# A table of 1237 numbers takes over the order in which a fused attention and MLP-mixer kernel emits its operations

## The chip, the cores and the metric

The kernel runs on one core of a Trainium2 chip. The metric is the device time of one execution in microseconds (us). A core has TensorE (PE in the profile, its weight loads PEld), VectorE (DVE), ScalarE (ACT), GpSimd (POOL) and SyncE (SP), which here issues every DMA. Each engine works through its own instructions in the order in which the program lists them and waits on semaphores for the others.

A difference of about 0.2% (0.8 us) is what a measurement of this kernel can tell from no change.

## The reference

```python
x  = A_x                                   # 1 x 2048 x 512
xn = layernorm(x)
s  = A_ref(xn, A_wqkv, A_wo)               # sliding local attention, 32 heads of 16, 8 keys at distance 2
g  = silu(B_ref(xn, B_w1, B_b1, B_w2, B_b2))   # layernorm, 512 -> 1376, gelu, -> 512
return x + s * g
```

In `A_ref` each position s looks at keys and values s, s-2, ..., s-14; scores are scaled by 1/4, masked where the index is negative, and softmaxed over the eight. `B_ref` layer-normalises its input a second time.

## The kernel before

The 2048 positions are split into even and odd ones (`DIL = 2`, index `c`), each half into `NI = 8` tiles of 128 rows, and the 32 heads into `NHB = 4` groups of 8 (index `hb`). All matmuls are fp16 pairs: a number is a high and a low half, a product is three matmuls (high by high, low by high, high by low), so each operand is first scaled by a power of two, rounded (`hi`) and its remainder computed (`lo`).

- **Start.** `load` issues the DMAs of x, the qkv weights and w1. Row statistics of each x tile are taken on DVE (`ln0`, L576, L577, L631); POOL raises them to the power -1/2 (L635); `y0` applies them (L661 on ACT, L665 on POOL, L668 on DVE), transposes the tile on PE (L683) and writes its halves to `yT` (L687, L689, L690), or sends it through a DMA transpose (L675). For tiles 6 and 7 `direct` multiplies centred x by unrounded weights in fp32 (L617). `scale_q` takes sums of squares of a weight group on ACT (L514), PE adds them over the partitions (L430), DVE makes the scale (L441 to L459); `prep_q` writes the weight halves (L536 on ACT, L543 on DVE, L470 and L471 on POOL). While PE has nothing to do, 24 matmuls on a constant run (`WAKE`, L1169).
- **Eight units** (`c`, `hb`). `qkv` fills U[u % 2] with 8 tiles of 12 matmuls of 384 columns (L746), each scaled out of PSUM by ACT (L763) or DVE (L759), then DMAs on SP build the halo of the neighbouring rows (L771). `attention` runs almost wholly on DVE in instructions of 2048 elements a partition (L805, L808, L863, L858), with its softmax exp on ACT and parts of its sums on POOL (L873, L883).
- **MLP** of four chunks of 512 rows, 11 slices f each, poured between the units: `mlp1` (12 matmuls, L1016), gelu and high half on ACT (L1033, L1036), low half on DVE (L1038), `mlp2` (12 matmuls into the four banks z0 to z3, L1052), silu on ACT (L1063, L1068), and for three chunks a store to scratch (`gd`). The weights w2 get their scale from sums of squares on ACT (L421, L1232) which PE adds over the partitions (L435).
- **End.** `wo_first` multiplies the even half by `wo` (L929). `wo_last` does the odd half (L961) in nine parts, seven tiles and the last one in two halves: nine matmuls of the first three head groups, then three of the last; DVE multiplies by the gate (L993), DVE or POOL adds x (L1000, L997), SP stores the tile (L1002). The x tiles of this stage are loaded by L983 into the seven-buffer ring `R_f`.

What sets the order: every step is handed to a planner (`Plan.add`) with an engine, an assumed duration, its reads and writes and a priority. `Plan.issue` then simulates the engines: each time it takes the operation that can start first by the assumed durations, priority breaking near ties, gives it buffers of its rings, and notes it. At the end the operations are emitted in that order; a ring buffer goes to the operation that comes first in this order.

Of the kernel before, what the change touches and what calls it, by code (L numbers as in the profile page):

```python
# [66 lines left out]
W2LATE = 6  # L67

BEFORE_W1 = (0, 1, 4, 5)

class Buf:

# [24 lines left out]
class Plan:  # L97
# [9 lines left out]
    def add(self, eng, dur, fn, reads=(), writes=(), prio=None, table=None, nbytes=0,  # L107
# [14 lines left out]
        o.n = len(self.ops)  # L122
        o.eng, o.dur, o.fn, o.table, o.nbytes = eng, dur, fn, table, nbytes
        o.port, o.rate, o.issue, o.tail = port, rate, issue, tail
        o.prio = self.prio if prio is None else prio
        o.preds, o.succs, o.bufs = set(), [], []
# [95 lines left out]
    def issue(self):  # L222
        self.start()
        engs = {o.eng: [] for o in self.ops}
        for o in self.ops:
            if not o.npred:
                engs[o.eng].append(o)
        order = []
        while len(order) < len(self.ops):
            best = None  # L230
            for e, cand in engs.items():
                lst = []
                for o in cand:
                    t = self.earliest(o)
                    ok = True
                    for b in o.bufs:
                        if b.slot is None:
                            f = min(b.ring.free)
                            if f == float("inf"):
                                ok = False  # L240
                                break
                            t = max(t, f)
                    if ok:
                        lst.append((t, o))
                if lst:
                    t0 = min(x[0] for x in lst)
                    t, o = min((x for x in lst if x[0] <= t0 + (WINDOW if x[1].prio > PURG else WURG)),
                               key=lambda x: (x[1].prio, x[1].n))
                    if best is None or (t, o.prio) < (best[0], best[1].prio):
                        best = (t, o)  # L250
            if best is None:
                raise RuntimeError("no operation can be placed")
            t, o = best
            engs[o.eng].remove(o)
            for b in o.bufs:
                if b.slot is None:
                    r = b.ring.free
                    b.slot = r.index(min(r))
                    r[b.slot] = float("inf")
            end = self.place(o, t)  # L260
            for b in o.bufs:
                b.left -= 1
                b.end = max(b.end, end)
                if not b.left:
                    b.ring.free[b.slot] = b.end
            for x in self.done(o, end, MARGIN):
                engs[x.eng].append(x)
            order.append((t, o))
        self.end = max(self.free.values())
        for t, o in order:  # L270
            o.fn()
# [1095 lines left out]
```

## Time and profile before

| | |
|---|---|
| median of 3 runs | 414.9 us (414.75 to 414.92) |
| time of the profiled execution | 415.18 us |
| its span, first to last instruction | 413.4 us |
| mean granted TensorE clock | 0.999 |
| busy PE / DVE / ACT / POOL | 405.9 / 379.5 / 222.1 / 120.3 us |
| DMA moved | 46.41 MB |

The span is 1.8 us under the profiled execution's time. A busy time counts a stretch once even where instructions overlap. In a list of waits each row gives the waiting engine and line, what released it, and the total, count and longest of the waits. In a timeline, a row starts with start and duration in us, merges equal neighbours (x4), and puts the idle time before it and its releaser in brackets.

### The profile page before, as it was taken

How to read it: one execution, taken by the hardware profiler on the slowest of the kernel's cores; microseconds unless marked ns; L12 is line 12 of the kernel's file. 1: busy time of each engine (PE TensorE's matmuls, PEld its weight loads, DVE VectorE, ACT ScalarE, POOL GpSimd, SP SyncE). 2: the span in 40 equal slices, each digit the busy share in tenths (PEclk: the TensorE clock that was granted, in tenths of full speed). 3: DMA queues.
4: the chain of work that ended last, by engine and by line, in shares of the span. 5: the costliest groups of instructions: out<-in, count | busy, mean ns of one | idle time of the engine just before them, and what ended most of it. 6: DMA issues, size and time to landing. Idle time of an engine off the chain costs nothing.

```text
span 413.4 us, 5554 instructions
## 1 busy us (share of the span) xinstructions
PE 405.9 (98%) x2083; PEld 206.6 (50%) x2083; DVE 379.5 (92%) x379; ACT 222.1 (54%) x353; POOL 120.3 (29%) x131
## 2 busy tenths in 40 slices
PE   8799999999999999999999999999999999999996
PEld 5555544445654455445544554455455544444443
DVE  4996989998999999989998999999999998999954
ACT  4699899994549655843384252225212393263500
POOL 3834002004380425042504330434033404520021
PEclk9999999999999999999999999999999999999999
DMA  8958717030045137720172034223604244007133
GB/s 281 397 112 258 235 61 230 0 128 1 1 142 152 28 93 183 149 46 2 48 221 75 0 102 116 68 86 88 205 7 122 88 111 145 0 18 238 23 102 131
DMA packets 47211, 46.41 MB, mean 112 GB/s; under 512 B 31785, under 2 KB 32225, under 8 KB 46673
## 3 DMA queue, kind: packets, MB, share of 16 engines
q1 hardware_dynamic: 47184, 46.06, 37.6%
q8 instruction: 16, 0.26, 0.3%
q14 instruction: 11, 0.08, 0.1%
HBM read 24.06 MB, written 7.34 MB: 76 GB/s over the span
## 4 chain that ended last, share of the span: by engine, by line
PE 92%; ACT 3%; issue 1%; DVE 1%; POOL 1%; ACTq 0%
PE z L1052 28%; PE ps L1016 28%; PE ps L746 25%; PE ps L929 5%; PE ps L961 2%; PE z L961 2%; PE pl L746 1%; ACT w L421 1%; PE pl L961 1%; ACT f L673 1%; ACT yT L687 0%; ACT wq L536 0%; POOL wq L471 0%; POOL rb L635 0%; ACT prod L661 0%
## 5 line engine op out<-in xcount | busy, mean ns | idle before, releaser
L1016 PE MATMUL ps<-yT,w 128*128 128x512 f16 (+1 forms) x528 | 120.4, 379 | 0.0
L746 PE MATMUL ps<-wq,yT 128*128 128x384 f16 x708 | 117.0, 326 | 0.2 <-DVE U L759 0.2
L1052 PE MATMUL z<-w,h 128*128 128x512 f16 x480 | 110.4, 379 | 0.0
L746 PEld LDWEIGHTS <-yT 128*128 128x128 f16 x744 | 72.5, 98 | 49.2 <-issue 1.0
L1016 PEld LDWEIGHTS <-w 128*128 128x128 f16 (+1 forms) x528 | 52.8, 100 | 61.0
L805 DVE TENSOR_TENSOR prod<-U 128x2048 f32<-128x2048 f32 x32 | 73.2, 2286 | 2.2 <-POOL prod L883 0.7
L1052 PEld LDWEIGHTS <-h 128*128 128x128 f16 x480 | 46.6, 98 | 55.5 <-issue 0.3
L808 DVE TENSOR_REDUCE L<-prod 128x128 f32<-128x2048 f32 x32 | 73.0, 2281 | 0.4
L1033 ACT ACTIVATE ps<-ps,b1T,hsc 128x512 f32<-128x512 f32 (+1 forms) x44 | 32.9, 748 | 73.4 <-PE ps L1016 72.2
L863 DVE TENSOR_TENSOR prod<-pl,U 128x2048 f32<-128x2048 f32 x28 | 63.2, 2283 | 4.2 <-POOL prod L873 4.1
L763 ACT ACTIVATE U<-ps,cs 128x384 f32<-128x384 f32 x54 | 31.2, 580 | 65.2 <-PE ps L746 65.2
L873 POOL TENSOR_TENSOR prod<-prod,prod 128x2048 f32<-128x2048 f32 x7 | 31.7, 4531 | 113.8 <-DVE prod L863 99.6
L883 POOL TENSOR_TENSOR prod<-prod 128x1024 f32<-128x1024 f32 x14 | 32.9, 2349 | 0.0
L882 POOL COPY gate<-prod 1x1 f32<-1x1 f32 x21 | 5.5, 264 | 91.0 <-DVE prod L805 82.2
L1038 DVE SCALAR_TENSOR_TENSOR h<-ps,hsc,h 128x512 f16<-128x512 f32 x40 | 29.6, 741 | 1.7 <-ACT h L1036 1.4
L1036 ACT ACTIVATE h<-ps,hsc 128x512 f16<-128x512 f32 x40 | 27.3, 684 | 1.3 <-PE z L1052 0.4
L929 PE MATMUL ps<-wo,oT 128*128 128x512 f16 x96 | 21.7, 379 | 0.0
L858 DVE TENSOR_TENSOR prod<-prod,prod 128x2048 f32<-128x2048 f32 x9 | 20.5, 2282 | 0.0
L1033 ACT ACT_TABLE_LOAD x10 | 12.8, 1283 | 8.6 <-PE ps L1016 8.5
L883 POOL TENSOR_TENSOR prod<-prod,prod 128x1024 f32<-128x1024 f32 x7 | 16.4, 2347 | 0.0
L961 PEld LDWEIGHTS <-oT 128*128 128x128 f16 x108 | 10.6, 98 | 10.4
L929 PEld LDWEIGHTS <-oT 128*128 128x128 f16 x96 | 9.4, 98 | 11.2
(179 smaller groups left out, 377.8 us busy)
## 6 DMA issues: line engine op xcount, KB each, us to landing
f<-in_A_x_dram SPq DMA_DIRECT2D x31, 256.0 KB, 3.5
U<-U SPq DMA_DIRECT2D x16, 392.0 KB, 4.0
gd<-f SPq DMA_DIRECT2D x12, 256.0 KB, 3.4
prod<-in_A_x_dram SPq DMA_DIRECT2D x8, 256.0 KB, 6.9
oT<-in_B_w_dram SPq DMA_DIRECT2D x2, 1024.0 KB
yT<-in_B_w_dram SPq DMA_DIRECT2D x2, 1024.0 KB, 7.9
f<-gd SPq DMA_DIRECT2D x8, 256.0 KB, 2.7
out_dram<-f SPq DMA_DIRECT2D x8, 256.0 KB, 2.8
```

The costliest lines, as they stand in the source:

```text
L746: nc.tensor.matmul(b.t[:, 0:384], y[:, s, k, o:o + P], wq[:, hb, t, k], start=(n == 0), stop=(n == 11))
L763: act(384, lambda i=i, b=b: nc.scalar.activation(U3[:, i:i + 31:15, :], b.t[:, 0:384].rearrange("p (t e) -> p t e", t=3), AF.Identity, sca ...
L805: dve(2048, lambda p2=p2, g=g: nc.vector.tensor_tensor(p2(), q, slots(Ut, KH, 2 * g), op=ALU.mult), qk + [("kh", ub, 0), ("kh", ub, 1), (" ...
L808: dve(2048, lambda pr=pr, g=g: nc.vector.tensor_reduce(L3()[:, 2 * g:2 * g + 2], pr.t.rearrange("p (r f d) -> p r f d", r=2, d=DH), AX.X, ...
L863: dve(2048, lambda: nc.vector.tensor_tensor(pr.t.rearrange("p (r f d) -> p r f d", r=2, d=DH), A3()[:, 2 * g:2 * g + 2].rearrange("p r (f ...
L873: pool(4.75, lambda: nc.gpsimd.tensor_tensor(acc.t, acc.t, p1.t, op=ALU.add), [acc, p1], [acc])
L883: nc.gpsimd.tensor_tensor(x.t[:, 0:1024], x.t[:, 0:1024], y(), op=ALU.add)
L929: nc.tensor.matmul(b.t, oT[:, hb, i // 4, s, i % 4], wo[:, t, hb], start=(hb == 0 and n == 0), stop=(hb == last and n == 2))
L961: nc.tensor.matmul(b.t[:, cols], oT[:, hb, i // 4, s, i % 4], wo[:, t, hb, cols], start=(start and hb == 0 and n == 0), stop=(stop and hb ...
L1016: nc.tensor.matmul(b.t[0:M], w1[:, s, f * 512 + k * M:f * 512 + (k + 1) * M], yT[ch][:, t, k], start=(n == 0), stop=(n == 11))
L1033: act(512, lambda: nc.scalar.activation(b.t[0:M], b.t[0:M], AF.Gelu_apprx_tanh, bias=b1T[0:M, f:f + 1], scale=hsc[0:M, 1:2]), [b, ("b1T",) ...
L1052: nc.tensor.matmul(z.t, hl[s][0:K, t * P:(t + 1) * P], w2[0:K, w, f], start=(f == 0 and n == 0), stop=(f == NF - 1 and n == 2))
```

## The change

`ORDER` lists all 1237 operations of the planner by number. `Plan.issue` takes them one after the other from this table in place of choosing; the choosing loop is then never entered. Operations, their durations for the planner, shapes, engines and data are the same. What differs is the order on each engine's queue, and which buffer of a ring an operation gets.

```diff
+ORDER = (
+    0, 1, 19, 2, 3, 4, 5, 6, 7, 8, 9, 10, 33, 32, 108, 116, 115, 130, 111, 124, 110, 114, 129, 112, 127, 20,
...
+    1197, 893, 1216, 1202, 1232, 1207, 1222, 1212, 1227, 1236, 1217,
+)
...
-        order = []
+        order, fixed = [], [self.ops[n] for n in reversed(ORDER)]
         while len(order) < len(self.ops):
             best = None
-            for e, cand in engs.items():
+            if fixed:
+                o = fixed.pop()
+                t = max([self.earliest(o)] + [min(b.ring.free) for b in o.bufs if b.slot is None])
+                assert not o.npred and t < float("inf")
+                best = (t, o)
+            for e, cand in engs.items() if best is None else ():
```

The line numbers of the changed kernel are 64 higher than before up to `Plan.issue` and 69 higher behind it (L514 is L583, L993 is L1062). Three places follow.

ACT at the start. `prod_93` holds the weights of the first head group, `U_87` those of the second, `wq` the fp16 weights; `z_146` is the PSUM bank with the transposes of x tile 0, and `yT_82` receives it. Before:

```order
L514 ACT_TABLE_LOAD
L514 ACTIVATE wq,s_122<-prod_93 128x768 x2
L536 ACTIVATE wq<-prod_93,qsc 128x384 x4
L514 ACTIVATE wq,s_124<-U_87 128x768
L687 CAST yT_82<-z_146 128x4x128
L514 ACTIVATE wq,s_124<-U_87 128x768
L659 ACTIVATE rb_151<-pb_150,rb_151 128x1
```

The same queue now:

```order
L583 ACT_TABLE_LOAD
L583 ACTIVATE wq,s_121<-prod_93 128x768 x2
L605 ACTIVATE wq<-prod_93,qsc 128x384 x2
L583 ACTIVATE wq,s_123<-U_87 128x768
L605 ACTIVATE wq<-prod_93,qsc 128x384
L583 ACTIVATE wq,s_123<-U_87 128x768
L605 ACTIVATE wq<-prod_93,qsc 128x384
L756 CAST yT_82<-z_146 128x4x128
```

Both sums of squares of the second head group now stand ahead of the fourth weight chunk of the first group and of the first cast of x.

DVE at the end. `ps`, `z` are PSUM banks, `U_86` holds gate, product and result of the odd half, `f` the x tiles; rows of 128x256 are the halves of the last tile. Before:

```order
L993 SCALAR_TENSOR_TENSOR U_86<-z_144,osc,U_86 128x512
L1000 TENSOR_TENSOR U_86<-U_86,f_101 128x512
L993 SCALAR_TENSOR_TENSOR U_86<-z_145,osc,U_86 128x512
L1000 TENSOR_TENSOR U_86<-U_86,f_102 128x512
L993 SCALAR_TENSOR_TENSOR U_86<-z_146,osc,U_86 128x256
L1000 TENSOR_TENSOR U_86<-U_86 128x256
L993 SCALAR_TENSOR_TENSOR U_86<-ps_139,osc,U_86 128x256
L1000 TENSOR_TENSOR U_86<-U_86 128x256
```

Now:

```order
L1062 SCALAR_TENSOR_TENSOR U_86<-ps_139,osc,U_86 128x256
L1069 TENSOR_TENSOR U_86<-U_86 128x256
L1069 TENSOR_TENSOR U_86<-U_86,f_96 128x512
L1069 TENSOR_TENSOR U_86<-U_86 128x256
L1062 SCALAR_TENSOR_TENSOR U_86<-z_145,osc,U_86 128x512
L1069 TENSOR_TENSOR U_86<-U_86,f_100 128x512
```

The last part is now a whole tile (bank z20, tile 6) and no longer half a tile; PE's last twelve matmuls are likewise those of bank z20, with 512 columns, and no longer those of bank ps0, with 256.

SP at the end. `o160` goes through a DMA transpose into `oT` for the last head group; rows of `out_0_dram` are the stores. Before:

```order
L983 DMA f5_101<-in_A_x_dram 128x512
L983 DMA f6_102<-in_A_x_dram 128x512
L983 DMA U0_86<-in_A_x_dram 128x512
L851 DMA_TRANSPOSE oT_88<-o160_105 128x8x128 x2
L1002 DMA out_0_dram<-U0_86 128x512 x7
L1002 DMA out_0_dram<-U0_86 128x256 x2
```

Now:

```order
L920 DMA_TRANSPOSE oT_88<-o160_105 128x8x128 x2
L1052 DMA f3_99<-in_A_x_dram 128x512
L1071 DMA out_0_dram<-U0_86 128x512
L992 DMA out_0_dram<-f1_97 128x512
L1071 DMA out_0_dram<-U0_86 128x512
L1071 DMA out_0_dram<-U0_86 128x256
L1071 DMA out_0_dram<-U0_86 128x512 x4
L1071 DMA out_0_dram<-U0_86 128x256
L1071 DMA out_0_dram<-U0_86 128x512
```

A store of the even half (L992, from buffer f1) has moved to the end, so one buffer of the ring is missing and the load of an x tile into f3 (tile 4) has moved behind the transposes, where it must wait for the add that reads the x tile now in f3. The last three stores are those of tile 6, of the second half of tile 7, and of tile 4; by the table they stand in this order, so the store of the part that is computed last is no longer the last of the queue: two more stand behind it.

58 rows, old and new, of the table ORDER are left out of this document.

## The prediction

> **What bounds the kernel now.** I read the page's engine shares first, then PE's waits, then the busy times by stretches.
>
> ```profile
> PE 405.9 (98%) x2083; PEld 206.6 (50%) x2083; DVE 379.5 (92%) x379; ACT 222.1 (54%) x353; POOL 120.3 (29%) x131
> ...
> PE z L683 <- POOL prod L665: 1.6, 1, 1.6
> PE z L683 <- DVE prod L668: 0.4, 1, 0.4
> PE ps L746 <- DVE U L759: 0.2, 1, 0.2
> ...
> L1169 PE MATMUL z<-fours 128*128 128x256 bf16 x24 | 5.3, 389 | 1.2 <-DVE fours L365 1.2
> ...
> 0.00:10.00 10.00, 8.61 (x35) 5.20 (x36) 4.43 (x15) 4.23 (x8) 3.39 (x12) 1.00 0.80 277
> 10.00:20.00 10.00, 7.87 (x47) 5.19 (x48) 9.57 (x29) 6.42 (x14) 8.16 (x9) 1.00 1.04 411
> 20.00:30.00 10.00, 9.81 (x61) 5.73 (x59) 9.72 (x25) 9.97 (x17) 4.73 (x4) 1.00 0.48 105
> 30.00:120.00 90.00, 89.92 (x474) 45.77 (x472) 82.64 (x103) 70.30 (x133) 22.05 (x24) 1.00 0.37 116
> 120.00:160.00 40.00, 39.96 (x210) 20.35 (x208) 38.84 (x29) 26.82 (x43) 13.11 (x14) 1.00 0.40 103
> 160.00:240.00 80.00, 80.00 (x416) 40.76 (x414) 75.67 (x55) 42.51 (x61) 24.84 (x26) 1.00 0.34 86
> 240.00:360.00 120.00, 120.00 (x610) 59.78 (x609) 116.70 (x88) 45.41 (x60) 36.19 (x33) 1.00 0.33 98
> 360.00:400.00 40.00, 40.00 (x187) 18.45 (x186) 34.59 (x31) 16.45 (x21) 5.70 (x11) 1.00 0.29 80
> 400.00:414.00 14.00, 9.76 (x58) 5.39 (x55) 7.36 (x12) 0.00 (x0) 2.16 (x2) 0.95 0.41 150
> ```
>
> PE is the bound. In the windows the first number is the length and the next PE's busy time: from 30 to 400 us it is busy 369.88 of 370 us, although DVE is close behind it (348.4 us of the same 370). PE's waits are the three rows of 1.6, 0.4 and 0.2 us and the 1.2 us before the first constant matmul, 3.4 us in all. The 24 constant matmuls (5.3 us) fill holes of the start. An order can't shorten the matmuls; so from 30 to 400 us a new order can only lose, and what can be won is at the start (those waits, and holes that the constant matmuls cover) and behind the last matmul.
>
> **The start.** Two chains must meet before PE's stream of L746 can run: x tile 0 (statistics, POOL, transposes, cast) and the four high chunks of the first weight group.
>
> ```profile
> 8.32 0.13 DVE L441 TENSOR_SCALAR ssq<-z 128x1 f32<-128x1 f32 x1
> ...
> 8.80 0.68 DVE L576 BATCH_NORM_STATS2 bn<-prod 128x6 f32<-128x512 f32 x1
> 9.52 0.18 DVE L577 BATCH_NORM_AGGREGATE mv<-bn 128x2 f32<-128x6 f32 x1
> ...
> 8.92 2.13 ACT L536 ACTIVATE wq<-prod,qsc 128x384 f16<-128x384 f32 x4 [1.15 <-DVE qsc L459]
> 10.96 0.83 ACT L514 ACTIVATE wq<-U 128x768 bf16<-128x768 f32 x1
> ...
> 13.55 0.59 ACT L687 CAST yT<-z 128x512 f16<-128x512 f32 x1 [1.67 <-PE z L683]
> 14.03 0.85 ACT L514 ACTIVATE wq<-U 128x768 bf16<-128x768 f32 x1
> ...
> 17.25 0.54 DVE L668 TENSOR_SCALAR prod<-prod,mv,rb 128x512 f32<-128x512 f32 x1
> ...
> 10.73 2.08 POOL L665 TENSOR_SCALAR prod<-prod,mv,rb 128x512 f32<-128x512 f32 x1
> ...
> 12.86 0.66 PE L683 MATMUL z<-ident,prod 128*128 128x128 f32 x4 [1.65 <-POOL prod L665]
> 13.35 2.75 PE L617 MATMUL z<-prod,U 128*128 128x384 f32 x8
> ...
> 15.96 0.81 PE L746 MATMUL ps<-wq,yT 128*128 128x384 f16 x4
> ...
> 17.84 1.85 PE L683 MATMUL z<-ident,prod 128*128 128x128 f32 x12 [0.40 <-DVE prod L668]
> ...
> f<-in_A_x_dram SPq DMA_DIRECT2D x31, 256.0 KB, 3.5
> U<-in_A_wqkv_dram SPq DMA_DIRECT2D x2, 384.0 KB
> ```
>
> Now tile 0's statistics come ahead of the weight scale on DVE: they start at 8.32 in place of 8.80, so POOL's L665 ends at about 12.81 - 0.45 = 12.4 and the transposes are 0.45 us early. The scale pays: its first instruction (L441) starts 0.9 us of statistics and 0.1 us behind 8.32, at 9.3, and so the first L536 at 8.92 + 1.0 = 9.9. From there ACT's new order runs two L536 (2 x 0.53), L514 (0.9 with its read-out), the third L536: 12.4. Then stands the second L514, which needs the last load of the second weight group. That load is the twelfth: eight tiles of x of 256 KB and four pieces of weights of 384 KB are 3.67 MB, of which 2.77 MB move in the first 10 us at 277 GB/s and the rest at 411 GB/s, an estimate of 12.2 us. The trace shows it present at 14.03. I take the middle, 13.1. So L514 runs 13.1 to 14.05, the fourth L536 to 14.6, the cast to 15.2, where before it ended at 14.14.
>
> PE's first L746 needs that cast: 15.2 against 15.96 before. But PE has by then done only four of the eight instructions of L617 on bank z; the other four (1.3 us) follow, so it stands at 15.2 + 1.3 = 16.5 where before it stood at 15.96: 0.55 us behind. Two constant matmuls that now stand in the full stream add 0.2 us each. Against this the waits of 0.40 and 0.2 us and the 0.1 us that the windows lack from 30 us on go: tile 2's normalisation (L668) no longer stands behind four others on DVE, nor its POOL step behind the weight remainder, and is done at about 15 in place of 17.79. Sum 0.55 + 0.4 - 0.7 = **+0.3** with rounding; with the load at 12.2 it is -0.6, with 14.0 it is +1.2. These are the bounds.
>
> One more early gate: PE's sum for the scale of w2 (L435).
>
> ```profile
> 52.97 1.90 ACT L421 ACTIVATE w<-yT 128x2048 bf16<-128x2048 f32 x1
> ...
> 56.58 0.17 PE L435 MATMUL z<-s,fours 128*128 128x5 bf16 x1
> ```
>
> It stood at 56.58 behind an ACT pass over 1 MB that ended at 54.9. The table puts it some 8 us earlier in PE's queue, at about 48 us, and has moved both 1 MB loads ahead of the halo DMAs and both ACT passes ahead of the first gelu. Followed through ACT's queue by the durations of the trace, the second pass ends at about 48.1, so PE, which can pass nothing here, waits 0 to 2 us, by whether the second 1 MB has landed by 46. I take **+0.3**.
>
> **The middle.** One row gives the size of DVE's long instructions:
>
> ```profile
> L805 DVE TENSOR_TENSOR prod<-U 128x2048 f32<-128x2048 f32 x32 | 73.2, 2286 | 2.2 <-POOL prod L883 0.7
> ```
>
> 233 of PE's 395 operations stand elsewhere relative to the others, but the matmuls' sum is the same. What cover there is: DVE must have each low half (L1038) done before PE reaches `mlp2`, and each bank read before PE writes it again. DVE, at 348.4 of 370 us, has 6% to spare. Where I set DVE's work ahead of such a step against PE's work ahead of its reader, before and now, the closest of the new pairs stand within 1.4 us of each other on either side of zero (PE's L746 into the bank that L1038 of slice 8 of the second chunk still reads, near 118 us). Bounds: 0, as in the windows now, to 2 us, about one of DVE's 2.29 us instructions in the way. I take **+0.1**, nearer to the row that holds now.
>
> **The end.** Here the order decides the time directly.
>
> ```profile
> 408.29 1.47 PE L961 MATMUL ps<-wo,oT 128*128 128x256 f16 x12
> ...
> 407.18 0.75 DVE L993 SCALAR_TENSOR_TENSOR U<-z,osc,U 128x512 f32<-128x512 f32 x1 [1.11 <-PE z L961]
> 407.97 0.69 DVE L1000 TENSOR_TENSOR U<-U,f 128x512 f32<-128x512 f32 x1
> ...
> 409.80 0.48 DVE L993 SCALAR_TENSOR_TENSOR U<-ps,osc,U 128x256 f32<-128x256 f32 x1 [0.29 <-PE ps L961]
> 410.32 0.42 DVE L1000 TENSOR_TENSOR U<-U 128x256 f32<-128x256 f32 x1
> ...
> 372.19 3.70 SPq L983 DMA_DIRECT2D f<-in_A_x_dram x7
> ...
> L1002 SPq DMA_DIRECT2D out_dram<-U x9: 332/333/344, 399.6 to 410.8; - x9
> ...
> DMA to landing us min/median/max: 1.7/2.0/2.0
> ```
>
> Before: PE ends at 409.76; DVE's two instructions take to 410.74; the last store, of 128 KB, is issued at 410.8, 1.0 us behind PE, and lands 1.7 us later (the least of the nine): 2.7 us behind PE. Now the last part is a whole tile: 0.04 + 0.75 + 0.04 + 0.69 = 1.55 us from PE's end to the issue of its store. Behind that store two others wait on SP's queue, though both are ready before: tile 7's second half is added before tile 6 on DVE, and tile 4's add on POOL (L997) ends, by the same steps backwards from PE's end, about 1.7 us before it. SP issues seven ready DMAs in 3.70 us, one in about 0.45 (3.27 between first and last, by six), so the third store goes out at 1.55 + 0.8 to 0.9 = 2.4 us and lands 2.0 us later: 4.4 us behind PE. That is 4.4 - 2.7 = **+1.7**. Bounds: if SP issues in 0.33 (the issue's own length) and the stores don't hinder each other, +1.5; if the third also loses to its neighbours the 0.3 us by which 256 KB land later than 128 KB, +2.0. If only the larger last part counted and the two others cost nothing: 0.55 + 0.3 = +0.85. Tile 4's late load is covered: it goes out behind an add some 8 us before PE's end, takes 3.5 us (the median row of these loads above), and is wanted 3 us before PE's end.
>
> [...]
>
> **Sum.** 0.3 + 0.3 + 0.1 + 1.7 = +2.4 us on a span of 413.4, that is 415.8. The profiled execution took 415.18, 0.28 above the median of the runs, so the forecast for the median is 414.9 + 2.4 = **417.3 us**.
>
> **Rivals.**
>
> 1. *The start wins more than the end loses.* Tile 2 and the DMA-transposed tiles are ready earlier; if the load that blocks ACT lands by 12.2, and the first L746 starts near 14.3 with tile 2's transposes behind it, PE gets back the 1.65, 0.40 and 0.2 us waits and some of the 5.3 us of fillers: -2.2 to -2.8. With the end at +0.85 to +1.7 this gives 413 to 414.4. The point that decides it is whether L746 runs without a break from 14.3 us or earlier. For: POOL's L665 was the longest wait of PE. Against: ACT's queue as shown, and 411 GB/s from 10 to 20 us, which no order betters. Faster: 0.10; between, within 0.2% (414.1 to 415.7): 0.12.
> 2. *DVE becomes the bound in the middle.* It is at 94% there; three or four low halves behind a 2.29 us instruction each, at 0.5 to 1.5 us a time, cost PE 2 to 4 us: 419 to 421.5. For: 143 of DVE's 335 operations have moved. Against: before, an order with as many close pairs had no wait at all. 0.15.
> 3. *The clock.* PE's granted clock is 1.00 through the start, with a pause of 1.65 us in it. The new order has fewer fillers behind 5 us; should PE fall to half speed for some 3 us while it has real work, that is 1.5 us more, 419. [...] 0.03.
>
> That the change does nothing is excluded: the queues differ as shown.
>
> **How the numbers follow.** Forecast as summed (415.7 to 419): 0.60. With rivals 2 and 3 slower has 0.78, same 0.12, faster 0.10. The range takes the start at -0.6 and the end at +0.85, with nothing for gate and middle (415.15, taken as 415.0) and on the other side 2 us of waits in the middle on top of the forecast (419.4); outside lie most of rival 1's wins and the worst of rival 2.
>
> **What would show it.** In the profile after: the last L961 on 512 columns, with three stores issued 1.5 us and more behind it, and about 5.4 us from PE's end to the span's end (3.6 before); the cast L756 at 14 to 16 us behind a L583 that waits for a DMA; 24 fillers as before; PE's busy time of 370 us between 30 and 400. It is wrong if PE's waits from 30 us on come to more than 2 us, if L746 runs unbroken from before 15 us, or if the last stores land within 3 us of PE's end.

## The result and the profile after

The changed kernel takes 430.0 us (median of 4 runs, 429.3 to 431.4) against 414.9 us (4 runs, 414.8 to 415.6): a ratio of 1.036, 95% interval 1.034 to 1.039. The forecast was 417.3 with a range to 419.4: the direction was right, the size was not. The profiled execution took 430.36 us.

First the engines' busy times on the page of the new kernel, then PE's waits (total, times, longest):

```profile
PE 410.7 (96%) x2083; PEld 207.0 (48%) x2083; DVE 392.4 (92%) x379; ACT 219.3 (51%) x352; POOL 124.1 (29%) x131
...
PE ps L815 <- DVE h L1107: 3.7, 3, 3.0
PE z L1121 <- DVE h L1107: 1.7, 2, 1.1
PE ps L499 <- ACT wq L583: 1.6, 1, 1.6
PE z L504 <- ACT w L490: 1.4, 1, 1.4
```

DVE is busy for 392.4 us where it was busy for 379.5, with the same 379 instructions. And PE, which had no wait over 0.2 us behind its start, now waits for low halves (L1107; L1038 before) and at two sums for weight scales. By stretches (PE busy, PEld, DVE, ACT, POOL, then PE's granted clock):

```profile
30.00:100.00 70.00, 66.76 (x339) 32.81 (x338) 63.32 (x79) 57.31 (x107) 14.06 (x13) 1.00 0.48 143
100.00:190.00 90.00, 90.00 (x467) 45.76 (x466) 88.18 (x76) 51.65 (x84) 29.30 (x28) 1.00 0.27 66
190.00:280.00 90.00, 85.66 (x435) 42.86 (x434) 80.13 (x55) 38.05 (x57) 25.68 (x26) 0.98 0.34 90
280.00:400.00 120.00, 118.62 (x595) 58.57 (x594) 116.62 (x86) 46.07 (x61) 35.36 (x38) 1.00 0.31 86
```

PE lacks 3.2 us in the first stretch, 4.3 in the third, 1.4 in the fourth: 9.0 of 370 us, where it lacked 0.12. In the third its clock falls as well. The end, on PE, and how SP's last stores go out:

```profile
420.30 2.75 PE L1030 MATMUL z<-wo,oT 128*128 128x512 f16 x12
...
423.87 0.69 DVE L1069 TENSOR_TENSOR U<-U,f 128x512 f32<-128x512 f32 x1
...
421.61 4.28 SPq L1071 DMA_DIRECT2D out_dram<-U  x7
```

PE ends at 423.05 (before: 409.76) and the span at 428.6 (413.4): 5.5 us of tail, where there were 3.6. Of the 15.2 us, PE's end carries 13.3 and the tail 1.9.

**The longest wait, followed back.** PE's 3.0 us is the wait of a projection (L815) for the bank that one low half still reads. DVE's instructions ahead of that low half, and POOL's:

```profile
215.75 4.49 DVE L932 TENSOR_TENSOR prod<-pl,U 128x2048 f32<-128x2048 f32 x2
220.15 1.27 DVE L917 SCALAR_TENSOR_TENSOR o<-prod,osc,o 128x1024 f16<-128x1024 f32 x1
225.83 2.29 DVE L932 TENSOR_TENSOR prod<-pl,U 128x2048 f32<-128x2048 f32 x1 [4.40 <-POOL prod L942]
...
238.04 2.29 DVE L874 TENSOR_TENSOR prod<-U 128x2048 f32<-128x2048 f32 x1
240.25 0.75 DVE L1107 SCALAR_TENSOR_TENSOR h<-ps,hsc,h 128x512 f16<-128x512 f32 x1
...
220.41 5.39 POOL L942 TENSOR_TENSOR prod<-prod,prod 128x2048 f32<-128x2048 f32 x1 [10.20 <-DVE prod L932]
...
241.05 5.25 PE L815 MATMUL ps<-wq,yT 128*128 128x384 f16 x21 [2.97 <-DVE h L1107]
```

Two products (L932) feed POOL's sum. The ring `prod` has three buffers: the sum holds two, and the third is read by L917 of the slice before. On the chip L917 was through with it at 221.42 us, but the next product had been given a buffer of the sum: buffers are handed out by the planner's clock, and by that clock L917, which stands behind the sum in the table, waits for the sum's end, so that a buffer of the sum is free first. The product therefore stood 4.40 us for POOL, and everything behind it on DVE, the low half at 240.25 among it, came late. Before, L848 (L917 here) stood at 206.6 us, 12.8 ahead of the sum, so that the third buffer was free, and two low halves and a product filled the time of the sum; DVE stood for 1.02 us there:

```profile
224.00 2.29 DVE L863 TENSOR_TENSOR prod<-pl,U 128x2048 f32<-128x2048 f32 x1 [1.02 <-POOL prod L873]
```

**Where DVE's extra 12.9 us come from.** Instructions by line and form, before and then after (busy, mean ns of one, idle ahead):

```profile
L863 DVE TENSOR_TENSOR prod<-pl,U 128x2048 f32<-128x2048 f32 x28 | 63.2, 2283 | 4.2 <-POOL prod L873 4.1
L848 DVE SCALAR_TENSOR_TENSOR o<-prod,osc,o 128x1024 f16<-128x1024 f32 x7 | 9.0, 1281 | 0.6 <-ACT o L846 0.6
L920 DVE TENSOR_TENSOR f<-f,f 128x512 f32<-128x512 f32 x8 | 6.5, 824 | 0.0
L713 DVE TENSOR_TENSOR f<-f,f 128x512 f16<-128x512 f32 x8 | 6.5, 810 | 0.0
```
```profile
L932 DVE TENSOR_TENSOR prod<-pl,U 128x2048 f32<-128x2048 f32 x28 | 63.6, 2283 | 6.4 <-POOL prod L942 6.0
L917 DVE SCALAR_TENSOR_TENSOR o<-prod,osc,o 128x1024 f16<-128x1024 f32 x7 | 14.8, 2111 | 0.0
L782 DVE TENSOR_TENSOR f<-f,f 128x512 f16<-128x512 f32 x8 | 9.5, 1186 | 0.0
L989 DVE TENSOR_TENSOR f<-f,f 128x512 f32<-128x512 f32 x8 | 8.7, 1083 | 0.1
...
353.21 4.50 DVE L917 SCALAR_TENSOR_TENSOR o<-prod,osc,o 128x1024 f16<-128x1024 f32 x1
352.12 4.51 POOL L942 TENSOR_TENSOR prod<-prod,prod 128x2048 f32<-128x2048 f32 x1 [10.19 <-DVE prod L932]
```

The products keep their 2283 ns. But L917, L782 and L989 went up by 5.8, 3.0 and 2.2 us in sum (and one L549 of the weights by 1.9), and it is single instructions: the last two rows show an L917 of 1.28 us that lasts 4.50, to 1.08 us behind the end of the sum beside which it began. Four instructions are held so (4.71, 3.88, 3.50 and 4.50 us in place of 0.68 and 1.28). Before, two were, L713 and L920, for 1.52 and 1.82 us. Beside POOL's seven sums DVE thus lost 10.7 us more in held instructions, and by the rows of L932 1.9 us more (6.0 for 4.1) in waits.

### The profile page after: what moved, and what is told of

The parts are those of the page before. It is cut to its first block, busy times and chain, and to the rows that moved or that the text cites. A ratio compares the mean times of both kernels' runs of the same rounds, so it can differ in the third digit from the quotient of the medians.

```text
span 428.6 us, 5536 instructions
## 1 busy us (share of the span) xinstructions
PE 410.7 (96%) x2083; PEld 207.0 (48%) x2083; DVE 392.4 (92%) x379; ACT 219.3 (51%) x352; POOL 124.1 (29%) x131
## 5 line engine op out<-in xcount | busy, mean ns | idle before, releaser
L815 PE MATMUL ps<-wq,yT 128*128 128x384 f16 x708 | 123.3, 329 | 4.5 <-DVE h L1107 3.7
L1121 PE MATMUL z<-w,h 128*128 128x512 f16 x480 | 113.8, 379 | 1.7 <-DVE h L1107 1.7
L815 PEld LDWEIGHTS <-yT 128*128 128x128 f16 x744 | 73.1, 99 | 59.6 <-issue 9.1
L874 DVE TENSOR_TENSOR prod<-U 128x2048 f32<-128x2048 f32 x32 | 73.1, 2288 | 4.6 <-DMA U<-U 3.2
L932 DVE TENSOR_TENSOR prod<-pl,U 128x2048 f32<-128x2048 f32 x28 | 63.6, 2283 | 6.4 <-POOL prod L942 6.0
L942 POOL TENSOR_TENSOR prod<-prod,prod 128x2048 f32<-128x2048 f32 x7 | 34.4, 4915 | 79.3 <-DVE prod L932 68.5
L1107 DVE SCALAR_TENSOR_TENSOR h<-ps,hsc,h 128x512 f16<-128x512 f32 x40 | 29.3, 742 | 2.7 <-ACT h L1105 2.6
L927 DVE TENSOR_TENSOR prod<-prod,prod 128x2048 f32<-128x2048 f32 x9 | 20.6, 2285 | 0.1
L917 DVE SCALAR_TENSOR_TENSOR o<-prod,osc,o 128x1024 f16<-128x1024 f32 (+1 forms) x9 | 16.3, 1808 | 0.8 <-ACT o L915 0.8
L915 ACT ACTIVATE o<-prod,osc 128x1024 f16<-128x1024 f32 (+1 forms) x9 | 9.5, 1053 | 14.0 <-DVE prod L927 10.0
L1030 PEld LDWEIGHTS <-oT 128*128 128x128 f16 x108 | 10.6, 98 | 10.2 <-issue 0.2
```

Of the source, the lines that this page charges most:

```text
L815: nc.tensor.matmul(b.t[:, 0:384], y[:, s, k, o:o + P], wq[:, hb, t, k], start=(n == 0), stop=(n == 11))
L874: dve(2048, lambda p2=p2, g=g: nc.vector.tensor_tensor(p2(), q, slots(Ut, KH, 2 * g), op=ALU.mult), qk + [("kh", ub, 0), ("kh", ub, 1), (" ...
L932: dve(2048, lambda: nc.vector.tensor_tensor(pr.t.rearrange("p (r f d) -> p r f d", r=2, d=DH), A3()[:, 2 * g:2 * g + 2].rearrange("p r (f ...
L942: pool(4.75, lambda: nc.gpsimd.tensor_tensor(acc.t, acc.t, p1.t, op=ALU.add), [acc, p1], [acc])
L1030: nc.tensor.matmul(b.t[:, cols], oT[:, hb, i // 4, s, i % 4], wo[:, t, hb, cols], start=(start and hb == 0 and n == 0), stop=(stop and hb ...
L1107: dve(512, lambda: nc.vector.scalar_tensor_tensor(lo()[0:M], b.t[0:M], hsc[0:M, 2:3], hi()[0:M], op0=ALU.mult, op1=ALU.subtract), [b, hk], ...
```

## The experiments

Fourteen kernels ran, against the kernel before (414.8 to 415.2). Where an edit is one of order, its diff names the instructions on their engine.

### Which part of the table: e4_first, e5_rest

```diff
-ORDER = new
+ORDER = new[:445] + [n for n in old if n not in new[:445]]   # e4_first
+ORDER = old[:445] + [n for n in new if n not in old[:445]]   # e5_rest
```

> The new table up to its 445th operation (about 104 us), from there the order of before for all that is left. Theory A (losses add up stage by stage on PE): the start costs 1.0, the constant matmul of the scale of w2 (L504) 1.6 at 49 us and the sum for the third weight group (L499) 1.8 at 67 us; nothing is given back, so 414.9 + 4.4 = 419.3 (418.5 to 420.3). Rival B (the early part also leaves DVE's work in a worse state, and the rest waits for it as in the new kernel): 423 to 430. Rival C (PE's early waits are caught up by fewer waits later): 415 to 417.

> The order of before up to its 445th operation (about 101 us), from there the new table for all that is left. Theory A (losses of PE add up stage by stage, independent of each other): the new kernel's 15.1 us less what its first part cost, 4.4 us by its trace and 6.9 us by the run that had the first part alone, so 423 to 426. Rival B (the waits behind 190 us are a consequence of the early delay, since DVE's and PE's queues have been shifted against each other there): under 420, near 417 with the end's 1.9 us alone. In the trace: theory A expects PE's 3 us wait for a low half near 228 to 235 us and half a clock behind it, rival B neither.

Measured: 421.7 (419.5 to 423.6) and 428.3 (427.0 to 428.4). In e4_first PE waits 2.8 us at L504 and 2.2 at L499, and behind 90 us it has no wait at all, although it arrives 8 us late there: the order of before takes an early delay without passing it on. In e5_rest the late waits are there though its start is that of before:

```profile
239.23 3.04 PE L815 MATMUL ps<-wq,yT 128*128 128x384 f16 x9 [2.97 <-DVE h L1107]
```

So the late losses belong to the later rows of the table, not to what went ahead of them; rival B of both falls. Theory A's sizes were too small in both: 421.7 is 1.4 us over the upper end of its range for e4_first, where a half clock of 3.41 us at 71 us came on top in the profiled execution, and 428.3 is 2.3 us over it for e5_rest. The two differences (6.9 and 13.1) sum to more than 15.1: e5_rest waits another 2.5 us at the seam (117 to 124 us), so the split is good for a sign and not for a size.

### The early gates: e7_gates

```diff
 PE
-L504 z<-s,fours          (w2's scale, at 50.7 us)
 ... four groups of L815 and L1085
+L504 z<-s,fours
 SP
+L574 yT<-in_A_wqkv x2    (third weight group)
 L840 U<-U                (halo, waits to 58.7 us)
-L574 yT<-in_A_wqkv x2
```

> The new table with three moves before 70 us: PE's constant matmul for the scale of w2 (L504) stands some 2.6 us of PE work later, and the two loads of the third weight group (L574) go out on SP ahead of the halo transfer (L840) that blocks SP to 58.7 us. Theory A: PE's waits of 1.4 us at 49 us and of 1.6 us at 67 us go, 430 - 3.4 = 426.6, and the rest of PE's waits stays. Rival B (later waits take up what is gained, as PE arrives earlier at a DVE that is not earlier): 429 to 430.

Measured: 426.6 (426.0 to 428.2). Both gates are gone from PE's waits, and the long one stays:

```profile
PE ps L815 <- DVE h L1107: 3.7, 3, 3.0
PE z L1121 <- DVE h L1107: 2.0, 3, 1.1
```

The time is the expected one, but in part by luck. Matmul for matmul, the profiled execution is 0.4 us ahead of that of the new kernel at 18 us, 0.6 at 57 us and 2.5 at 73 us: without the wait at L504, PE stands 0.8 us a little later for low halves (L555 of w2 and L1107), so that gate gave almost nothing and the loads of the third weight group 1.9. Another 1.7 us come from the half clock at 242 us, which this execution did not have although its pause of 2.97 us is there.

### Held instructions, put in and taken out: e3_hits, e1_apart

```diff
 DVE of before, four places such as this (e3_hits)
 L917 ... of 330 us, now here:
 L932 prod<-pl,U        (second of the pair that starts POOL's sum)
 L1107 h<-ps,hsc,h
+L917 o<-prod,osc,o
 DVE of the new table, four places such as this (e1_apart)
-L782 f<-f,f
 L932 prod<-pl,U
 L1107 h<-ps,hsc,h
 L932 prod<-pl,U
+L782 f<-f,f
```

> The order of before with four DVE instructions moved a few places, each to 0.1 to 0.9 us behind the start of a POOL sum (L942): L782 to 137.5 us, L917 to 220.1, L989 to 299.6, L917 to 341.6 us. Theory A (held until POOL's sum ends): each lasts 4.1 to 4.7 us in place of 1.52, 1.28, 0.68 and 1.28; DVE's busy time 379.5 + 3 + 3.1 + 3.9 + 3.3 = 392 to 393; PE waits for low halves behind them, and the time rises by 4 to 9 us, to 419 to 424. Rival B (the order of the low halves is what costs; DVE's durations are those of before): DVE's busy time within 1 us of 379.5 and the time within 1 us of 415. A middle result, long instructions and a time under 416.5, would say that DVE's slack of 6% takes them up and that the new order lost elsewhere.

Measured: 422.4 (422.3 to 422.8), theory A. Each of the four ends 0.55 us (L782, L989) or 1.08 us (L917) behind its sum; DVE's busy time rose by 13.9 us, to 393.4. One of them and its sum:

```profile
348.33 5.18 DVE L917 SCALAR_TENSOR_TENSOR o<-prod,osc,o 128x1024 f16<-128x1024 f32 x1
...
347.92 4.51 POOL L942 TENSOR_TENSOR prod<-prod,prod 128x2048 f32<-128x2048 f32 x1 [13.14 <-DVE prod L932]
```

So four such places are enough to cost 7.6 us in an order that had no waits; a half clock of 3.41 us behind a wait of 2.7 us is part of that. One reservation: buffers are handed out by the planner's clock, so the four moves also give 200 operations another buffer (92 a PSUM bank `ps`), and the share of that in the 7.6 us is not shown.

> The new table with four DVE instructions moved one to three places back on DVE, so that none starts while a POOL sum (L942) runs or at least not at its start: L782 of 133.6 us, L917 of 182.5, L989 of 272.2, L917 of 353.2 us. Nothing else moves on any engine. Theory A (these instructions are held until POOL's sum ends): they fall from 4.71, 3.88, 3.50 and 4.50 us to 0.7 to 1.8 us, DVE's busy time from 392.4 to about 382 to 384, and since the DVE is what PE waits for behind 190 us, the time falls by 5 to 8 us to 422 to 425; the half-clock stretch at 242 us goes with the 3 us pause ahead of it. Rival B (the new places of the low halves alone make PE wait, however long DVE's instructions are): DVE's busy time may fall, but the time stays within 1 us of 430. Rival C (they are long for another reason, such as the place of their operands): DVE's busy time and the time stay.

Measured: 432.6 (432.2 to 435.1): slower than the new kernel, against all three theories. DVE's busy time did fall, to 380.3, but its idle time took the place of it:

```profile
L874 DVE TENSOR_TENSOR prod<-U 128x2048 f32<-128x2048 f32 x32 | 73.1, 2288 | 8.4 <-DMA U<-U 7.1
L932 DVE TENSOR_TENSOR prod<-pl,U 128x2048 f32<-128x2048 f32 x28 | 63.8, 2287 | 13.4 <-POOL prod L942 12.9
...
188.12 2.29 DVE L932 TENSOR_TENSOR prod<-pl,U 128x2048 f32<-128x2048 f32 x1 [3.38 <-POOL prod L942]
```

With L917 moved behind the product, the product waits 3.38 us for a buffer that POOL's sum reads, since L917 still holds the third: held or waiting, DVE stands to the end of the sum. And L782 feeds a DMA transpose (L784) that stands on SP ahead of two halo transfers (L840); all three went out 3.9 us later, and DVE waited 3.91 us for them at 149 us. My theory A was too narrow: the held instruction is one of two forms of the same loss. Here, too, 76 operations got another buffer.

### The place of the low halves: e6_low, e8_all

```diff
 DVE at 233 us
+L1107 h<-ps,hsc,h
 L874 prod<-U
 L877 L<-prod
 L874 prod<-U
-L1107 h<-ps,hsc,h
```

> The new table with two DVE instructions moved: one low half (L1107) goes ahead of three instructions of 2.29 us (L874, L877, L874) behind which it stood at 240.2 us though its input was there at 233.6, another goes ahead of one (L927) behind which it stood at 194.3 us, its input there at 191.5. The four held instructions stay where they are. Theory D (what costs is a low half that stands in DVE's queue behind work that nobody waits for, not the held instructions as such): PE's waits of 1.1 us at 195 and of 3.0 us at 238 us go, and with the latter the half clock (1.7 us): 430 - 5.8 = 424, and DVE stays at 390 or more. Rival E (DVE is short of time there, so the wait goes over to the next low half): 428 to 430.

> The new table with the two low halves moved, the three moves before 70 us, and the last stores in the order in which their data is ready, seven instructions in all. Theory (independent terms): 430 - 5.8 - 3.4 - 0.9 = 419.9. Rival (the moves serve the same slack and don't add up): 423 or more. Below 414.8 would beat both kernels; the start and the longer last part speak against it.

Measured: 428.7 (427.9 to 430.5) and 426.4 (426.1 to 427.4). Rival E holds for the most part. The 3.0 us wait and the half clock go, and other waits come, 1.2 us at 198 us among them:

```profile
PE ps L815 <- DVE h L1107: 1.9, 3, 1.2
...
PE ps L998 <- DVE h L1107: 1.4, 1, 1.4
```

Part of that can be the edit's own: the two moves also give 108 operations another buffer, 98 of them a bank. So these runs don't tell the place of a low half from the bank it reads. e8_all is where e7_gates is, so its rival holds and the terms don't add up.

### DVE's time beside POOL's sums: e9_ahead, e10_all, e12_dvesum

e9_ahead moves L917 ahead of the pair at three sums, and L782 and L989 back; e10_all adds the gates and the order of the stores.

```diff
 DVE at 217 us, one of three such places
 L932 prod<-pl,U
+L917 o<-prod,osc,o
 L932 prod<-pl,U
-L917 o<-prod,osc,o
 ACT at 337 us
+L915 o<-prod,osc
 L900 L<-L
 ...
-L915 o<-prod,osc
```

> The new table with six moves around five of POOL's sums (L942). Each sum reads two of the three buffers of the ring prod; the third is free for DVE's next product (L932) only once L917 of the slice before has read it. Three L917 (at 182.5, 220.2 and 353.2 us), which stand behind the pair of products that starts the sum, go ahead of the pair's second product, as in the order of before; for the last one ACT's half of it (L915) is moved ahead too. L782 of 133.6 us and L989 of 272.2 us go three places back. Theory F (DVE stands through POOL's sums, held in an instruction or waiting for a buffer, and it is this lost time that makes the low halves late): DVE's busy time 381 to 384, its idle time ahead of L932 no more than 6 us (after: 6, with four instructions held; with the four moved back: 13), PE's waits of 1.1 us at 195 and of 3.0 us at 238 us and the half clock behind it gone, 430 - 6 = 424 (422.5 to 425.5). Rival E (the low halves' places alone, DVE's lost time doesn't matter): PE's 3.0 us wait stays, and the time stays at 428 or more.

> The six moves around POOL's sums together with the three moves before 70 us and the order of the last stores. Theory (the terms add up): 424 - 3.4 - 0.4 = 420.2. Rival (what is gained early is taken by later waits, as the kernel with all the earlier moves showed, 426.4): 424 or more.

Measured: 434.9 (433.5 to 435.3) and 431.7 (431.2 to 432.4): both missed. The edit made waits of its own. L917 cannot go ahead without ACT's half (L915), which came at 220.8 us and kept DVE 2.2 us; and where L915 was moved too, it waited for its only buffer, ahead of the softmax:

```profile
343.43 1.15 ACT L915 ACTIVATE o<-prod,osc 128x1024 f16<-128x1024 f32 x1 [6.43 <-DMA oT<-o]
...
346.55 0.69 DVE L902 TENSOR_REDUCE mx<-L 128x64 f32<-128x512 f32 x1 [4.08 <-ACT L L900]
...
355.04 3.36 PE L815 MATMUL ps<-wq,yT 128*128 128x384 f16 x10 [5.08 <-DVE h L1107]
```

The wait at 238 us did fall to 1.6 us, without half clock, as theory F has it; but 136 operations got another buffer, and new waits of 1.7, 1.1 and 5.1 us outweigh it. So these two runs decide nothing. The gates and the order of the stores together were worth 3.2 us here. So the sum itself was taken away, with order, buffers and banks as they are:

```diff
-pool(4.75, lambda: nc.gpsimd.tensor_tensor(acc.t, acc.t, p1.t, op=ALU.add), [acc, p1], [acc])
+if u in (2, 3):
+    add(2048, lambda: acc.t, lambda: p1.t, lambda: acc.t, [acc, p1], acc)
+else:
+    pool(4.75, lambda: nc.gpsimd.tensor_tensor(acc.t, acc.t, p1.t, op=ALU.add), [acc, p1], [acc])
```

> The new table as it is, with two of POOL's seven sums (L942 of the slices whose sums run at 180.8 and 220.4 us) done on DVE in the same places of the order, 2.29 us each; buffers and banks of all operations as in the new kernel. That takes away at these two places both what holds L917 (3.88 us at 182.5) and what keeps L932 waiting for a buffer (4.4 us at 221.4). Theory F (DVE's time lost beside POOL's sum makes the low halves late): DVE reaches the low half that PE waits for at 240.2 us some 2.5 us earlier although it does 4.6 us more of work; PE's waits of 1.1 us at 195 and 3.0 us at 238 us shrink to under 1 us together, the half clock behind goes: 430 - 4.9 = 425 (424 to 426.5). Rival E (DVE has no time there whatever POOL does): the waits stay or grow, 430 to 433.

Measured: 425.9 (425.4 to 427.6), as theory F has it, though PE's waits at 195 and 238 us fell from 4.0 to 1.8 us together and not to under 1. DVE at the same place as above (the sum is its L927 row), and PE's waits (L1110 is the low half here):

```profile
220.07 2.29 DVE L927 TENSOR_TENSOR prod<-prod,prod 128x2048 f32<-128x2048 f32 x1
222.28 1.28 DVE L917 SCALAR_TENSOR_TENSOR o<-prod,osc,o 128x1024 f16<-128x1024 f32 x1
223.47 2.28 DVE L932 TENSOR_TENSOR prod<-pl,U 128x2048 f32<-128x2048 f32 x1
...
PE ps L815 <- DVE h L1110: 1.7, 2, 1.2
```

The product starts at 223.47 where it started at 225.83, the low half at 237.89 where it stood at 240.25, PE's wait is 1.2 us, and no half clock follows. DVE does two instructions more, 394.3 us in all, and the kernel is 4.1 us faster: what counted was when DVE is free, not how much it does.

### Do the terms add up: e13_best, e14_four, e15_low

```diff
-if u in (2, 3):
+if u in (1, 2, 3, 4, 6):   # e13_best, with the edits of e7_gates and e2_stores
+if u in (1, 2, 3, 4):      # e14_four, the same otherwise; e15_low: and that of e6_low
```

> Five of POOL's seven sums done on DVE (all but the first, and the one at 310.8 us where DVE was neither held nor kept waiting over 1.6 us), with the three moves before 70 us and the order of the last stores. Theory F: at the five sums DVE lost 4.0, 2.6, 4.4, 3.6 and 3.2 us in the new kernel and does 2.29 us in place of it, so that the small waits from 275 us on shrink too: 425 - 3.4 - 0.4 - 1 = 420 (418.5 to 422). Rival: 424 or more.

> Four of POOL's sums done on DVE in place of five (the one at 352 us stays on POOL), with the three moves before 70 us and the order of the last stores. Theory F: with the fifth, a sum of 2.29 us stood on DVE ahead of two low halves that PE waits for, which gave a wait of 2.86 us at 348 us and 3.4 us at half clock behind it; without it the wait there is 0.5 us and the time 425.9 - 2.3 - 1.7 = 421.9 (420.5 to 423). Rival: the time stays at 424 or more, then the terms of the gates and of the sums don't add up, and more is lost to something that the waits don't show.

> The same with the two low halves moved ahead as well. Theory F: now that DVE has the time, the moves pay: the remaining waits of 0.7 us at 195 and 1.2 us at 238 us go, 421.9 - 1.8 = 420.1 (419 to 421.5). Rival E (a low half that is moved up only passes the wait to the next one, as without the sums on DVE): within 0.5 us of the kernel without the two moves.

Measured: 425.9 (424.5 to 426.3), 423.1 (422.7 to 424.1) and 424.3 (423.9 to 425.8). The first is a miss for theory F (its rival holds), the second is 0.1 us over F's range, the third fits neither side. In e13_best the fifth sum stood on DVE ahead of the two low halves that PE needed next:

```profile
345.19 2.29 DVE L927 TENSOR_TENSOR prod<-prod,prod 128x2048 f32<-128x2048 f32 x1
347.40 1.40 DVE L1110 SCALAR_TENSOR_TENSOR h<-ps,hsc,h 128x512 f16<-128x512 f32 x2
...
348.20 4.11 PE L815 MATMUL ps<-wq,yT 128*128 128x384 f16 x15 [2.86 <-DVE h L1110]
```

Without it the time is 2.7 us less (e13_best also gives 24 later operations another bank, e14_four none). Gates, sums and stores together thus gave 430.0 - 423.1 = 6.9 us, where singly they gave 3.4 + 4.1 + 0.1. That comes within a microsecond, but is no proof that the terms are independent: the 1.7 us of the half clock are in both 3.4 and 4.1, and e14_four has two sums more on DVE than e12_dvesum. e15_low refutes the hope that the low halves' moves pay once DVE has time: 1.2 us slower than without them, with 1.15 us of wait again at 196 us, on a bank given out otherwise.

### The last stores: e2_stores

```diff
 SP
+store of tile 7's second half
+store of tile 4
 store of tile 6
-store of tile 7's second half
-store of tile 4
```

> The new table with the last three stores in the order in which their data is ready: the stores of tile 7's second half and of tile 4 go out ahead of the store of tile 6. Theory A (stores queued behind one that isn't ready): from PE's end to the span's end 4.5 to 4.7 us in place of 5.55, the time 0.9 us lower, 429.1. Rival B (the landing of the last whole-tile part sets the end whatever stands behind it): unchanged, 430.0 and 5.5 us.

Measured: 429.9 (429.0 to 432.2) against 430.0, no difference that the runs can tell; by its profile 5.1 us from PE's end to the span's end in place of 5.5. That is 0.4 where theory A wanted 0.9. Two things are left in the tail, the whole last tile and the crowd: seven stores go out within 3.6 us (4.3 in the new kernel), and the 256 KB ones land 2.4 us behind their issue (2.0 before).

None of the fourteen beats the kernel before, and none points to an order that would: PE has no wait behind its start there.

## Why the prediction was wrong, point by point

- **The start** (+0.3): the size was right, by luck. The cast ends at 15.53 (forecast 15.2), and by an estimate from the matmuls done PE is 0.7 to 1.0 us behind at 30 to 40 us, within the bounds. But the wait that was forecast did not come: the second L583 at 13.64 found its load there. What came late was the weight scale, whose sum on PE (L499) stood to 10.41 behind L686 and constant matmuls, so that the first L605 started at 11.28 and not at 9.9. And the first L815 started at 15.59, not 16.5: the last four L686 stand behind it.

```profile
11.28 1.12 ACT L605 ACTIVATE wq<-prod,qsc 128x384 f16<-128x384 f32 x2 [2.72 <-DVE qsc L528]
...
13.64 0.83 ACT L583 ACTIVATE wq<-U 128x768 bf16<-128x768 f32 x1
```

- **The gate of w2's scale** (+0.3, 0 to 2): the wait was right in kind: 1.44 us in this execution. Of the six other kernels with this place unchanged, e4_first has 2.8 us, e6_low 0.3 and four have none. It is not the second 1 MB that decides: ACT stood 1.49 us for a smaller load of w2 (L1301 at 46.16) ahead of both passes. And e7_gates shows that without the wait PE loses almost as much a little later. One more gate of that kind was not in the sum: the two loads of the third weight group. On SP they were moved behind a halo transfer that waits for evacuations, in a piece of SP's queue that I had not followed:

```profile
37.55 21.63 SPq L840 DMA_DIRECT2D U<-U  x3
...
61.28 0.59 SPq L574 DMA_DIRECT2D yT<-in_A_wqkv_dram  x1
...
68.71 0.16 PE L499 MATMUL ps<-s,fours 128*128 128x1 bf16 x1 [1.61 <-ACT wq L583]
```

- **The middle** (+0.1, 0 to 2): this is the step that failed. It set DVE's work ahead of each low half against PE's work ahead of its reader, and took DVE's durations and waits from the trace of before. Both depend on the order. Beside POOL's sums DVE lost 12.6 us more than before (10.7 held, 1.9 waiting), over half of the 21.6 us it had to spare from 30 to 400 us, and from 190 to 400 us PE lost 5.7 us in waits (the windows above) and 1.7 to the half clock behind the longest of them: 7.4 us where 2 was the bound, and the sign of error that the prediction itself had named. e12_dvesum, in which every operation keeps its buffers, shows that in the new table taking away the two sums ahead of the longest waits gives 4.1 us back; e3_hits shows that four held instructions put into the order of before can cost as much, other buffers included. What the buffers cost by themselves (the new table gives 633 operations another one than before) no run separates. Two things at hand could have warned. The trace of before has a held instruction, an L713 of 0.68 us that lasts 1.52, to 0.55 us behind POOL's sum:

```profile
140.32 1.52 DVE L713 TENSOR_TENSOR f<-f,f 128x512 f16<-128x512 f32 x1
...
136.74 4.55 POOL L873 TENSOR_TENSOR prod<-prod,prod 128x2048 f32<-128x2048 f32 x1 [14.00 <-DVE prod L863]
```

  And the kernel's planner knows of it: POOL's sums and DVE's L713, L848 and L920 are marked `port`, products and low halves are not, and `earliest` puts an operation so marked behind the one before it (`portfree`). The choosing loop went by that; a fixed table does not.
- **The end** (+1.7): right in sum, 1.9 by the profile, with two errors that offset each other. Of its working, the share of the queued stores was too large (0.4 by e2_stores), that of the longer last part and of the crowd of stores too small.
- **Rival 2** (DVE becomes the bound, 419 to 421.5) was right in kind, and the step on the middle named the right reader, a projection into a bank that a low half still reads (near 118 us, where it cost nothing). Its mechanism was too small: it priced low halves behind one long instruction each, and in e6_low and e15_low moving them up did not pay. **Rival 3** (the clock) came, at 1.7 us (3.41 us at half clock) near its price of 1.5, but behind a wait in the middle and not at the start.
- The three terms that came within their bounds (start 0.7 to 1.0, gate 1.4, end 1.9) make some 4 of the 15.2 us; about 11 were lost where the sum had +0.1 or nothing: 7.4 in the middle, 1.6 at L499, the rest not assigned. The runs took back 6.9 us in all. Of the 7.6 us of span that e14_four's profile still lies above that of before, 1.4 is tail and 6.2 lies in the start and in waits of up to 1.2 us each; these were not taken apart further and stay open.

## What to carry to other kernels

A duration read from a trace holds for the order in which it was read: before moving an instruction, look at what runs on the other engines beside its new place, whether the two hold each other up, and which buffer of a ring it frees. A rule that the program keeps while it chooses an order (here `port`) is not kept by an order that is given to it. Three in-order queues (DVE, SP, ACT) pass a late instruction on to each other: most edits here that moved an instruction on DVE made another wait, while e12_dvesum, which took a cause away, did not. And follow each queue through to its end: a moved load behind a transfer that waits for some 20 us costs what no duration shows.

## What the runs showed of the hardware

- **DVE and POOL.** An L917, L782 or L989 that starts beside a running POOL sum (4.5 us, both inputs in SBUF) has nearly all of its work still to do when the sum ends: it ends 1.08 us behind it (L917, 1.28 us long elsewhere) or 0.55 us (the two others, 0.68 us elsewhere), in all eight cases (four in the new kernel, four in e3_hits), as do the two held before. L932 and L1107, which have an operand in PSUM, keep their means of 2283 and 742 ns beside the same sums (2292 and 739 to 751 in the new kernel; before, as L863 and L1038, 2277 to 2281 and 737 to 751). It works the other way round too: the sum at 220.41 lasted 5.39 us in place of 4.53, as an L917 had started 0.26 us ahead of it, and the sum at 310.81 lasted 6.44 us behind an L874. What in the hardware lies behind this, no run shows.
- **The clock.** After PE's pause of 2.97 us the new kernel ran 3.41 us at half clock (granted share 0.5, from 241.78 us); e7_gates had the same pause, to 238.56 us, and none. First row after, second e7_gates, each from about the pause's end:

```profile
241.00:246.00 5.00, 4.95 (x21) 2.55 (x21) 4.86 (x3) 0.58 (x1) 2.23 (x3) 0.66 0.00 0
```
```profile
238.00:246.00 8.00, 7.44 (x44) 4.30 (x44) 7.46 (x5) 1.85 (x3) 4.87 (x4) 1.00 0.01 2
```

  In the profiles of all kernels here, behind 20 us, 9 of 14 pauses of 2.1 to 5.1 us went with half clock (3.41 us of it, once twice that), and none of the shorter ones, the longest of them 2.0 us (e1_apart). One of 2.2 us went with it (e4_first, at 71 us), the 2.97 us of e7_gates did not; what decides, the runs do not show.
